# Split-head attention followed by routed experts on one core: batch 2's outputs and routing pulled into batch 3, gathers placed behind their experts' weights

## The chip, the cores and the metric

The kernel runs on one core of a Trainium2 chip. The metric is the time of one execution in microseconds (us), measured on the device. The parts of a core that matter here are these: PE (matrix multiply), DVE (VectorE), ACT (ScalarE), POOL (GpSimd, which here issues all casting, gathering and scattering DMAs), and 16 DMA engines that all queues share (see the prediction's citation of the Trainium skill). "Half clock" below means a granted clock of 0.50 in the profile's clock record. A "gather" reads rows of HBM by an index table, a "scatter" writes rows back by one.

A run counts as slow when it is over 1.5% above the fastest run of its kernel. Single runs of one kernel differ by several per cent here, mostly with the clock that PE was granted. The kernel before took from 200.9 to 213.4 us within one job, at mean clocks from 0.96 down to 0.88. Ratios are taken inside one job, on fast runs.

## The reference

Four batches of 768 tokens and 8 heads of 64 go through causal attention. Heads 0, 2 and 6 see all earlier keys. The others see 4 sink keys and a window of 64. The 3072 tokens of 512 features then go through 8 experts:

```python
skip_score = x @ w_skip                 # tokens at or below 0 are passed through
logits = xc @ w_gate                    # 8 experts
e_idx = np.argmax(logits, axis=1)       # one expert a token
gate_w = softmax(logits)[e_idx]
for e in range(E):
    h = np.maximum(xc[mask] @ w1[e], 0.0)       # 512 x 1024
    y[mask] = gate_w * (h @ w2[e])              # 1024 x 512
out[do_compute] = xc + y
```

## The kernel before

The attention output is written to `out` in HBM. Each expert has two slots of 128 tokens (t = 0, 1). Slot 0 is filled from batches 0 to 2 and slot 1 last. A slot's rows are gathered from `out` by an index table, computed, and scattered back. Attention runs batch by batch in six "slots" of work; the outputs of batch b-1 (`"o"`) and their transposes and gates (`"x"`) are interleaved with the scores of batch b.

```python
def trans(b, pr):                       # queries and keys of one pair of heads
    ...
    eng = nc.scalar.copy if name == "qT" and b else nc.vector.tensor_copy
    eng(t..., ps...)                    # PSUM -> SBUF
    ...
    elif pr:                            # small product for the sink keys: reads the key copy
        nc.vector.tensor_tensor(y..., t..., half, op=ALU.mult)

def outp(g):                            # output block g; one bank `av` until batch 3
    avo = oview(sp.tile(...) if g >= g0 else av)
    ...                                 # PE, then DVE divides, then SP stores to `out`

def route(c0):                          # a generator: go_on() runs its next stage
    ...                                 # DVE: maximum, one-hot `oh`, ...
    yield
    rp = tp.tile(sh, FP32, tag="t", name="rps")
    ...                                 # PE: rank matmuls, read `oh`
    yield ...                           # DVE: rank; POOL: product; PE: table `tb`; DVE: idg, idx

# experts, in order of issue on POOL
#   4 gathers t=0 | w2[3], w1[4], w2[4] | 4 gathers t=1 | w1[5] | gathers of 4 | w2[5]
#   | gathers of 5, 6, 7 | w1[6] | w2[6], w1[7] | w2[7] | scatters
```

The scatters are declared free of order among themselves. A scatter still waits for every gather issued earlier, because both use `out`.

The softmax here doesn't subtract the row's maximum and nothing guards it: scores larger than these inputs give would overflow.

## Time and profile before

| | before |
|---|---|
| median of the runs beside the changed kernel | 204.38 us (201.17 to 205.56, 4 runs) |
| profiled span, mean granted clock | 204.6 us, 0.950 |
| PE busy | 163.1 us (80%) |
| batch 3's first exponential | 75.23 us |
| first expert matmul | 121.94 us |
| last PE matmul ends | 194.9 us |
| first, last scatter issued | 160.58, 195.96 us |

PE and the DMA engines are both nearly full, and the tail behind PE's last matmul is 9.7 us. The views are in the prediction. A row of a timeline gives start, duration, engine, line, operation, output <- input, and in brackets how long the engine stood idle before it and what released it.

### The profile page before, as it was taken

To read this page: it belongs to the slowest core of one execution; us is meant where nothing else is said; L and a number is where in the kernel's file an instruction comes from. 1 tells how busy PE (TensorE), PEld (TensorE's weight loads), DVE (VectorE), ACT (ScalarE), POOL (GpSimd) and SP (SyncE) were. 2 spreads that over 40 slices of the span, in tenths; PEclk is the share of its full clock that TensorE was granted. 3 is DMA by queue.
4 is the path that set the end of the run, shared out by engine and by line. 5 is a ranking of instruction groups with operands and counts; after the bars stand their busy time and mean duration, and the time that the engine had idled before them with its cause. 6 is when DMAs were issued, how large, how long until landed. Compare 5 with 4: busy or idle time off the path is not lost. (4 is left out here: it accounts for less than half of the span.)

```text
span 204.6 us, 5665 instructions
## 1 busy us (share of the span) xinstructions
PE 163.1 (80%) x2422; PEld 116.7 (57%) x2422; DVE 111.9 (55%) x282; ACT 83.5 (41%) x116; POOL 85.1 (42%) x105
## 2 busy tenths in 40 slices
PE   5898878967788687886898688959988959999900
PEld 1455556746566565664777558648755727657400
DVE  5888877554957849574683626233345344344410
ACT  2067788855874558746121133212322422232000
POOL 8659711421861218412014801687632451145430
PEclk9999999999999999999669889988999999999985
DMA  5999999999899999999999899999999999942010
GB/s 164 174 172 157 180 196 214 222 181 229 139 182 228 240 216 246 225 190 243 215 235 272 222 171 238 208 302 239 239 258 181 208 210 211 278 155 79 23 67 3
DMA packets 53172, 39.97 MB, mean 195 GB/s; under 512 B 27976, under 2 KB 44360, under 8 KB 53136
## 3 DMA queue, kind: packets, MB, share of 16 engines
q0 software_dynamic: 49136, 32.43, 104.2%
q1 hardware_dynamic: 3728, 6.69, 9.7%
q8 instruction: 21, 0.34, 0.6%
q10 hardware_dynamic: 272, 0.39, 0.5%
q14 instruction: 15, 0.12, 0.2%
HBM read 56.66 MB, written 10.49 MB: 328 GB/s over the span
## 5 line engine op out<-in xcount | busy, mean ns | idle before, releaser
L433 POOL CAST x<-x 128x512 f16<-128x512 f32 x17 | 10.7, 627 | 43.3 <-DVE x L426 37.4
L344 ACT ACTIVATE at<-sps 128x1024 f16<-128x1024 f32 (+1 forms) x24 | 21.7, 918 | 11.6 <-PE sps L333 11.1
L685 POOL DMA_INDIRECT out_dram<-xg,idx x16 | 16.0, 1001 | 24.0 <-DVE xg L748 10.6
L731 PE MATMUL mhp<-mxT,w1t 128*128 128x128 f16 (+1 forms) x320 | 24.4, 238 | 0.7 <-ACT mxT L717 0.7
L731 PEld LDWEIGHTS <-w1t 128*128 128x128 f16 x320 | 22.6, 103 | 3.5 <-issue 1.1
L735 DVE TENSOR_SCALAR ht<-mhp 128x512 f16<-128x512 f32 x16 | 11.1, 691 | 23.3 <-PE mhp L731 20.3
L746 PE MATMUL myp<-w2t,ht 128*128 128x512 f16 x96 | 23.6, 380 | 0.0
L748 DVE SCALAR_TENSOR_TENSOR xg<-myp,tab,xg 128x512 f32<-128x512 f32 x16 | 12.0, 751 | 19.6 <-PE myp L746 18.2
L679 POOL DMA_INDIRECT xg<-out_dram,idg x16 | 16.4, 1025 | 10.5 <-DVE tab L536 4.8
L737 ACT ACTIVATE ht<-mhp 128x512 f16<-128x512 f32 x16 | 9.6, 597 | 26.5 <-PE mhp L731 21.1
L383 ACT ACTIVATE ats<-sps 128x1024 f16<-128x1024 f32 (+1 forms) x16 | 12.3, 808 | 14.6 <-PE sps L374 14.6
L746 PEld LDWEIGHTS <-ht 128*128 128x128 f16 x128 | 12.0, 99 | 10.3
L439 PE MATMUL xps<-ident,x 128*128 128x128 f16 (+1 forms) x96 | 12.9, 263 | 6.0 <-ACT qT L302 2.4
L302 DVE COPY kT<-tps 128x768 f16<-128x768 f16 x16 | 15.2, 951 | 3.5 <-PE tps L296 3.5
L333 PE MATMUL sps<-qT,kT 64*128 64x512 f16 (+3 forms) x96 | 15.1, 308 | 0.0
L328 PE MATMUL sps<-tri,idl 64*128 64x128 f16 x144 | 11.4, 221 | 3.3 <-ACT ats L383 2.7
L717 ACT COPY mxT<-mtp 128x512 f16<-128x512 f16 x11 | 6.2, 587 | 17.7 <-PE mtp L714 16.8
L426 DVE TENSOR_TENSOR x<-av,rec 128x512 f32<-128x512 f32 x18 | 12.5, 692 | 1.4
L349 ACT ACTIVATE at<-sps 128x1024 f16<-128x1024 f32 (+1 forms) x12 | 10.8, 916 | 5.0 <-PE sps L333 4.8
L114 POOL DMA_DIRECT2D va<-in_v_dram x8 | 11.4, 1426 | 2.7 <-DMA va<-in_v_dram 1.2
L446 DVE COPY xT<-xps 128x512 f16<-128x512 f16 x17 | 7.6, 446 | 7.2 <-PE xps L439 7.0
L517 POOL TENSOR_TENSOR mv<-ot,vals 128x192 f32<-128x192 f32 (+1 forms) x4 | 2.5, 618 | 21.7 <-DVE ot L511 21.7
(152 smaller groups left out, 341.5 us busy)
## 6 DMA issues: line engine op xcount, KB each, us to landing
out_dram<-x SPq DMA_DIRECT2D x24, 256.0 KB, 5.8
w1t<-in_moe_w_dram POOLq DMA_DIRECT2D x6, 1024.0 KB
w2t<-in_moe_w_dram POOLq DMA_DIRECT2D x6, 1024.0 KB
va<-in_v_dram POOLq DMA_DIRECT2D x8, 384.0 KB
qin<-in_moe_w_dram POOLq DMA_DIRECT2D x2, 1024.0 KB
kin<-in_moe_w_dram POOLq DMA_DIRECT2D x2, 1024.0 KB
qin<-in_q_dram POOLq DMA_DIRECT2D x2, 768.0 KB
kin<-in_k_dram POOLq DMA_DIRECT2D x2, 768.0 KB
```

What stands on the lines that cost most here:

```text
L114: nc.gpsimd.dma_start(out=y[:, x, :D], in_=vr[b, :, x])
L302: eng(t.rearrange("c (p n) -> c p n", n=NT), ps.rearrange("c n p -> c p n"))
L333: nc.tensor.matmul(ps[:, k, x:x + n], kT[b, pr][rows[i], j * P:(j + 1) * P], qT[b, pr][rows[i], q0:q0 + n], start=False, stop=True, skip_g ...
L344: nc.scalar.activation(both[b][:, :, o:o + w], ps[:, :, :w], ACT.Exp, scale=SCALE)
L383: nc.scalar.activation(both[b, pr][:, :, x0:x1], ps[:, :, :x1 - x0], ACT.Exp, scale=SCALE)
L426: nc.vector.tensor_tensor(x.rearrange("p c t d -> p t c d"), avo[:, :, :, :D], rec.unsqueeze(3).to_broadcast([P, 2, 4, D]), op=ALU.mult)
L439: nc.tensor.matmul(ps[:, s], x[:, s * P:(s + 1) * P], ident if x.dtype == FP16 else ident32, is_transpose=True, start=(s == 0), stop=(s == ...
L679: nc.gpsimd.indirect_dma_start(out=xg[e, t], out_offset=None, in_=out[:n, :], in_offset=bass.IndirectOffsetOnAxis(ap=idg[:, t, e:e + 1], a ...
L685: sc = nc.gpsimd.indirect_dma_start(out=out[:, :], out_offset=bass.IndirectOffsetOnAxis(ap=idx[:, t, e:e + 1], axis=0), in_=xg[e, t], in_o ...
L731: nc.tensor.matmul(hp[:, u], wts[e, 0][:, s, (f0 + u) * P:(f0 + u + 1) * P], xts[n][:, s], start=(s == 0 and u == 0), stop=(s == DS - 1 an ...
L746: nc.tensor.matmul(yp, hts[n][:, f, i * P:(i + 1) * P], wts[e, 1][:, f], start=(f == 0), stop=(f == FS - 1))
L748: nc.vector.scalar_tensor_tensor(xg[e, t], yp, tab[:, t, e, 1:2], xg[e, t], ALU.mult, ALU.add)
```

## The change

The intent: have batch 2's routing done by the end of batch 3, so that the first gathers go out early, the bridge between attention and experts is shorter, and no scatter stands between weight loads. The diff, cut to its core:

```diff
@@ trans
-            eng = nc.scalar.copy if name == "qT" and b else nc.vector.tensor_copy
+            eng = nc.scalar.copy if b and (name == "qT" or pr > 1) else nc.vector.tensor_copy
@@ outp
-        avo = oview(sp.tile(...) if g >= g0 else av)
+        avo = oview(sp.tile(...) if g >= g0 and i % 3 else av)
@@ gates: two blocks at a time, through a transpose bank and a ScalarE copy into SBUF
+        nc.scalar.copy(lg[:, g - 1:g + 1], ps)
@@ slots
-            (C(0), "x", "o", C(1), T(1)),
-            (C(2), "x", "o", T(2), C(3)),
...
+        if b + 1 == B:
+            return (
+                (C(0), "x", "o", C(1), "o", T(1)),
+                (C(2), "x", "o", C(3), "g", "x", T(2), lambda: begin(g0 - 2 * NT)),
+                (C(4), "x", "o", go_on, C(5), "o", H6(0), "g", go_on),
+                (H6(2), "x", "o", H6(4), "g", T(3), A, "x", go_on),
...
@@ last slot of batch 0
+            (S4, "o", X(3, pair, 0, 512), T(0, b + 1), V(0, 1, 2, 3), X(3, pair, 512, S)),
@@ bridge: the fills go; experts:
-    for e in range(FB):                 # before the first expert's second group
-        gather(e, 1)
-    load_half(5, 0, *qk)
-    gather(4, 0) ... load_half(5, 1, *qk) ... gathers of 5, 6, 7
     for n in range(len(units)):
...
         down(n, lambda: xin(n + 2))
         if n == 0:
+            gathers t=1; load_half(4, 1); gathers of 4; load_half(5, 0); load_half(5, 1); gathers of 5
         if n == FB:
             load_half(FB + 2, 1)
+            gathers of 6
+        elif n == FB + 1:
+            load_half(FB + 3, 0); load_half(FB + 3, 1)
+            gathers of 7
         if n > FB:
             scatters()
```

## The prediction

> **What bounds the kernel now.** I read the page's slices first, then stretches of time, then the chain of waits, then each engine's timeline. Rows of the page's part 2 (40 slices of 5.1 us, in tenths):
>
> ```profile
> PE   5898878967788687886898688959988959999900
> ...
> PEclk9999999999999999999669889988999999999985
> DMA  5999999999899999999999899999999999942010
> ```
>
> Two resources are nearly full: PE until 195 us, and the 16 DMA engines until 180 us. The stretches put sizes on it (columns: from:to, length, busy us of PE, PEld, DVE, ACT, POOL with counts, granted clock, DMA share, GB/s):
>
> ```profile
> 52.00:56.00 4.00, 3.03 (x74) 2.22 (x70) 3.68 (x6) 3.35 (x5) 3.87 (x4) 1.00 0.70 111
> ...
> 72.90:99.40 26.50, 20.61 (x472) 16.09 (x464) 17.34 (x47) 16.06 (x20) 9.34 (x12) 0.99 1.41 224
> 99.40:121.90 22.50, 17.82 (x247) 14.44 (x242) 12.15 (x43) 5.07 (x10) 7.52 (x8) 0.78 1.04 221
> ...
> 120.00:180.00 60.00, 52.05 (x510) 38.36 (x509) 24.35 (x56) 16.41 (x29) 25.02 (x26) 0.97 1.13 234
> ```
>
> I split the span by PE's timeline: batch 3's scores end at 99.4; a bridge (last outputs, their transposes, gates, routing, fills) runs to 121.9; experts run to 194.9; a tail of 9.7 us ends at 204.6. Batch 3 leaves PE idle 26.5 - 20.6 = 5.9 us. The bridge leaves it idle 4.7 us and runs it at clock 0.78. The queue ran low once in attention (111 GB/s at 52 to 56 us).
>
> The chain of waits in the experts (start, us, what):
>
> ```profile
> 136.77 10.04 DMA xg<-out_dram,idg
> ...
> 147.11 12.61 DMA xg<-out_dram,idg
> ...
> 164.60 16.08 DMA out_dram<-xg,idx
> ...
> 180.70 0.43 DVE mx L702
> ...
> 187.99 6.92 PE myp L746 x32
> ```
>
> Gathers take 10 to 13 us to land because they queue behind weight loads, and the scatter issued at 164.6 landed at 180.7, behind the last of them. POOL's timeline gives the order of issue:
>
> ```profile
> 156.00 0.89 POOL L119 DMA_DIRECT2D w2t<-in_moe_w_dram  x1 [1.87 <-PE myp L746]
> 160.58 1.07 POOL L685 DMA_INDIRECT out_dram<-xg,idx  x1 [3.70 <-DMA xg<-out_dram,idg]
> 161.96 1.05 POOL L685 DMA_INDIRECT out_dram<-xg,idx  x1 [0.30 <-issue]
> ...
> 195.96 0.98 POOL L685 DMA_INDIRECT out_dram<-xg,idx  x1 [0.75 <-DVE xg L748]
> ```
>
> The first scatter waited for the last gather to land (147.11 + 12.61 = 159.7): a scatter overwrites the tensor that gathers read. Later ones follow every 1.31 us (181.24, 182.61, 183.90, 185.18, 186.47). This will matter.
>
> **What the Trainium skill says.** "TensorE: Matmul & The Clock Gate", part 1: the array falls to half clock after about 3.4 us of idleness and needs about as long a busy stretch to recover. The trace agrees in kind: clock 0.57 in 98 to 106 us, 0.58 in 116 to 120, 0.57 in 136 to 140, each some us after PE gaps (1.42 at 96, 1.60 at 112, 2.36 at 133), though the gaps are shorter than the figure. "DMA: Bandwidth & Descriptors", "Issuing engines are not separate DMA queues": all DMAs interleave on the same 16 engines; hence the share of about 1 whoever issues. "Perfetto Trace Analysis", "DMA Instruction — SWDGE (GPSIMD)": the profiled end is that of descriptor generation, not of the data. The trace agrees: a gather shows 1.0 us on POOL and lands 10 us later. I therefore reckon POOL's issue time and the queue's time apart.
>
> **The change part by part.**
> 1. Batch 2's outputs move into slots 0 to 3 of batch 3, its transposes, gates and whole routing up to the last table into batch 3. From the bridge go: one fp32 transpose of 4 matmuls (99.40 to 100.31, 0.9 us; now fp16, which takes 0.23 from start to next start), two gates (2 x 0.13) and the 0.70 wait between them, the rank matmuls (102.38 to 103.21, 0.83), and the 0.49 wait for POOL's product. Sum 3.2 us. The 12 fp32 table matmuls (1.3 us, 97.42 to 98.84) leave batch 3's end for batch 1's routing, but batch 2's stay in the bridge.
> 2. Fills go: 2 at 118.65 (0.78 to the next start), 4 at 120.91 (0.88), and the 0.73 wait for DVE before the latter, because the first expert's matmuls no longer stand behind it. Sum 2.4 us.
> 3. Batch 3 takes up about 0.2 + 0.8 + 0.5 = 1.5 us more PE work. It has 5.9 us of idleness, mostly waits for ACT's exponentials, so I let half be hidden: +0.8 us. DVE loses two key copies of 0.95 us per batch to ACT, where one takes 0.80; both have room in batch 3 (17.3 and 16.1 of 26.5), so I count zero.
> 4. Gates go through a transpose bank and a small ACT copy, two blocks at a time: 12 copies of about 0.2 us (my guess from the 0.24 us of ACT's smallest activation), off the path except for the last. Zero.
> 5. The bridge's remaining work, 6 outputs and 6 fp32 transposes, is unchanged, and so are most of the DVE and POOL latencies behind the four gathers there. Fewer gaps may save some half-clock time: about 4 us of PE work stood at half clock at 101.3 to 105.4. I take 0.7 us.
> 6. Experts: the second-pass gathers are issued after the first unit, and the gathers of experts 4 to 7 behind their own weights. PE's order per unit hardly changes: 73.0 us before, 72.3 after, since the 1.3 us of table matmuls stay and one of several DVE stalls may go.
>
> PE path: 121.9 - 3.2 - 2.4 + 0.8 - 0.7 = 116.4 for the first expert; + 72.3 = 188.7; + 9.7 = 198.4 us.
>
> 7. The new order on POOL makes a second path. The last gather now stands behind the last weight, and all scatters behind it. Bytes: before, 60 us at 234 GB/s (14.0 MB) between 120 and 180 carried all remaining loads, gathers and some 7 scatters of 0.26 MB (1.8 MB, 7.8 us). Without them the queue would be done at 172.2. The earlier load of v, issued at the end of a batch, fills the hole at 52 to 56 (worth 4 x (219 - 111)/219 = 2 us, with 219 GB/s in 56 to 96); a new hole before the second-pass gathers may cost some of it back. I put the last gather's landing at 170.5 us. Then 16 scatters: 0.84 us to the first, 16 x 1.31 = 21.0, last issue done at 192.3; from there to the end took 204.6 - 196.94 = 7.7 us. Sum 200.0 us.
>
> So PE gives 198.4 and scatters 200.0, close enough that the outcome is the later of two uncertain times. The median before is 0.4 above the profiled span. My figure is 199.5 us, 2.7% below 205.0.
>
> **The rivals.** (a) *Scatters become the bound outright.* For: all 16 wait for the last gather, and DMA has been full until 180. If the queue doesn't run ahead, the gather lands at 176 and the end is 205.5: nothing gained. Against: no scatter competes with loads any more. (b) *PE decides, and the clock improves.* If the half-clock stretches (16 us at 0.57 together, about 6.9 us lost) mostly vanish with the gaps, the end is near 194. Against: gaps beside POOL's descriptor work remain, and the second-pass gathers sit between experts. (c) *Batch 3 does not hide the added work*: v of batch 3 landed only at 95.1 us (DVE waited 2.62 us for it), and DVE's queue now has those copies earlier, ahead of the transposes' evacuations. A stall of 3 us there is possible: about 202. Against: v is requested 5 us earlier, though the queue ahead of it is as long. (d) *The expert's gather arrives late*: the cast of expert 7 stood at 180.7; 5.5 us earlier is 175.2, against a landing at 170.5. Only if the landing slips by 5 us does PE stop.
>
> **Range and chances.** The terms of the PE path are uncertain by some 3 us, the landing by 4 us, and single runs before spread from 201.17 to 205.56. Range 194.5 to 205. Faster by over 2% means under 200.9: 0.62. Slower needs over 209.1, which would take a stall beyond (a): 0.05. The rest, 0.33.
>
> **What would show it.** In the changed profile: PE's first expert matmul near 116 us; no 512-column fills in the bridge; the table of batch 2 on PE just after output 2 of batch 3, and the first gather on POOL near 104 rather than 109.5; DMA near 200 GB/s or more at 52 to 56; the first scatter on POOL near 171, an unbroken train of scatters every 1.31 us up to the end, and the last one later than PE's last matmul by more than 2 us. I am wrong if the experts start after 119, if batch 3 lengthens by over 2 us, if the scatter train starts before 166 or after 176, or if the expert phase takes other than 70 to 75 us.

## The result, and the profile after

The changed kernel took 214.12 us (median; 212.77 to 215.26, 4 runs) against 204.38 us. The ratio is 1.057, with a 95% interval of 1.042 to 1.073. A ratio here is the mean time of one kernel's fast runs over that of the other's of the same rounds, so it is not quite the ratio of the medians.

| us | before | after | difference |
|---|---|---|---|
| batch 1's first exponential | 28.32 | 30.09 | +1.8 |
| batch 2's first exponential | 49.94 | 51.71 | +1.8 |
| batch 3's first exponential | 75.23 | 80.77 | +5.5 |
| batch 3's last score matmul ends | 99.4 | 108.1 | +8.7 |
| first expert matmul | 121.94 | 121.94 | 0.0 |
| last PE matmul ends | 194.9 | 198.5 | +3.6 |
| end | 204.6 | 212.2 | +7.6 |

The bridge became shorter by 8.7 us, and attention longer by as much. That both kernels start the experts at 121.94 us to the digit is chance. The loss in the total lies behind the first expert matmul: 3.6 us in the experts and 4.0 us in the tail.

The page's slices of the changed kernel (5.3 us each, in tenths):

```profile
PE   5899498889869997878998789999996939599400
...
PEclk9999969999975599999579999999998888999975
DMA  6999999989999999999965899999999999334320
```

The clock now dips inside attention (slices 6, 12 to 14, 20 and 21), the queue runs low in the bridge (slices 21 and 22), and PE has holes late in the experts. The stretches, with the columns as in the prediction:

```profile
57.16:60.57 3.41, 1.46 (x35) 0.99 (x32) 1.38 (x8) 2.83 (x5) 1.98 (x3) 0.99 2.04 200
60.57:74.22 13.65, 13.65 (x180) 10.00 (x179) 6.75 (x20) 6.08 (x10) 2.31 (x4) 0.50 1.17 234
...
108.10:121.90 13.80, 11.66 (x222) 10.37 (x219) 8.39 (x26) 5.04 (x12) 6.64 (x7) 0.99 0.60 185
110.00:112.00 2.00, 1.84 (x31) 1.66 (x30) 1.97 (x5) 0.00 (x0) 0.69 (x1) 1.00 0.00 0
...
120.00:180.00 60.00, 52.07 (x505) 37.16 (x504) 24.18 (x56) 17.23 (x31) 20.48 (x22) 0.94 1.10 216
```

In 3.41 us PE was busy 1.46 us, a share of 0.43. The next 13.65 us it was busy all the time at a granted clock of 0.50, which by the clock is about half of what it can do in that time. The queue stood empty from 110 to 112 us.

This is the longest of several half-clock stretches. Before PE's last matmul they are, in the changed kernel, 26.4 to 29.8, 60.5 to 74.1, 101.5 to 108.3, 162.9 to 166.3 and 173.1 to 176.5 us, 30.7 us together. In the kernel before they are 98.9 to 105.7, 116.0 to 119.4 and 136.5 to 139.9 us, 13.7 us together. So attention lost 1.8 us in batch 0, whose last slot was reordered; 3.8 us in batch 2 (29.1 us long against 25.3); and 3.2 us in batch 3 (27.3 against 24.2). The 7 us stretch near 100 us falls in the bridge before and at the end of attention after, so it moves some of the time from one row of the table to the other.

What made the gap before 60.5 us is in the waits of DVE and of PE before 120 us (engine and line, what it waited for, us in total, times, longest):

```profile
DVE skq L311 <- ACT kT L305: 13.0, 6, 2.8
```

```profile
PE rps L494 <- DVE oh L483: 2.7, 2, 2.0
```

The key copy went to ACT, but the small sink-key product that reads it stayed on DVE. ACT was busy with exponentials, and in the trace DVE did nothing until the copy had been made, 13.0 us in six waits. The routing's one-hot came directly behind the product, and PE's rank matmuls behind that; their timelines have it in batch 2:

```profile
58.95 0.16 DVE L311 TENSOR_TENSOR skq<-kT,half 128x8 f16<-128x8 f16 x1 [2.18 <-ACT kT L305]
```

```profile
60.45 0.21 PE L494 MATMUL rps<-oh,utri 128*128 128x48 f16 x1 [1.95 <-DVE oh L483]
```

The order on POOL at the end:

```profile
155.97 0.81 POOL L119 DMA_DIRECT2D w1t<-in_moe_w_dram  x1 [3.48 <-DMA qin<-in_moe_w_dram]
161.27 1.11 POOL L119 DMA_DIRECT2D w2t<-in_moe_w_dram  x1 [4.49 <-DMA kin<-in_moe_w_dram]
...
164.06 1.03 POOL L706 DMA_INDIRECT xg<-out_dram,idg  x1 [0.31 <-ACT mxT L744]
...
185.38 1.04 POOL L712 DMA_INDIRECT out_dram<-xg,idx  x1 [20.29 <-DMA xg<-out_dram,idg]
186.72 1.02 POOL L712 DMA_INDIRECT out_dram<-xg,idx  x1 [0.31 <-issue]
...
204.82 0.98 POOL L712 DMA_INDIRECT out_dram<-xg,idx  x1 [0.30 <-issue]
```

The last gather, issued at 164.06, was still on its way when POOL began a wait of 20.3 us for it. Then the 16 scatters left without a break, one each (204.82 - 185.38) / 15 = 1.30 us. The last was issued 6.3 us after PE had ended (198.5). On DVE's timeline the experts wait for gathers too, which no cast did before:

```profile
172.74 0.43 DVE L729 CAST mx<-xg 128x512 f16<-128x512 f32 x1 [2.92 <-DMA xg<-out_dram,idg]
...
184.01 0.43 DVE L729 CAST mx<-xg 128x512 f16<-128x512 f32 x1 [1.64 <-DMA xg<-out_dram,idg]
```

Casts waited 6.4 us in all, in pairs for experts 5, 6 and 7. The pairs became free at 161.5, 172.7 and 184.0, so some 11.3 us apart: the time in which the queue moves two weight halves and two gathers, while PE needs 7.9 us for such an expert before (176.40 to 184.33). The late experts ran at the queue's pace.

### The profile page after: what moved, and what is told of

Read it like the earlier page. It is cut to its first block, busy times and chain, and to the rows that moved or that the text cites. A ratio compares the mean times of both kernels' runs of the same rounds, so it can differ in the third digit from the quotient of the medians.

```text
span 212.2 us, 5669 instructions
## 1 busy us (share of the span) xinstructions
PE 170.8 (81%) x2416; PEld 120.1 (57%) x2416; DVE 107.6 (51%) x277; ACT 89.1 (42%) x134; POOL 86.3 (41%) x106
## 5 line engine op out<-in xcount | busy, mean ns | idle before, releaser
L437 POOL CAST x<-x 128x512 f16<-128x512 f32 x18 | 11.5, 641 | 48.0 <-DVE x L430 25.8
L712 POOL DMA_INDIRECT out_dram<-xg,idx x16 | 15.8, 990 | 24.9 <-DMA xg<-out_dram,idg 20.3
L758 PE MATMUL mhp<-mxT,w1t 128*128 128x128 f16 (+1 forms) x320 | 22.9, 230 | 1.2 <-ACT mxT L744 1.2
L758 PEld LDWEIGHTS <-w1t 128*128 128x128 f16 x320 | 21.1, 98 | 3.9 <-issue 1.4
L762 DVE TENSOR_SCALAR ht<-mhp 128x512 f16<-128x512 f32 x16 | 11.1, 691 | 15.7 <-PE mhp L758 15.7
L336 PE MATMUL sps<-qT,kT 64*128 64x512 f16 (+3 forms) x96 | 16.4, 322 | 1.0 <-DVE kT L305 1.0
L430 DVE TENSOR_TENSOR x<-av,rec 128x512 f32<-128x512 f32 x20 | 13.8, 692 | 1.5
L443 PE MATMUL xps<-ident,x 128*128 128x128 f16 (+1 forms) x96 | 11.6, 250 | 2.5 <-ACT qT L305 1.5
L331 PE MATMUL sps<-tri,idl 64*128 64x128 f16 x144 | 12.5, 233 | 0.9 <-ACT at L347 0.8
L741 PE MATMUL mtp<-ident,mx 128*128 128x128 f16 x44 | 4.8, 238 | 8.7 <-DVE mx L729 8.7
L282 PE MATMUL av<-esk,ident 128*128 128x512 f16 x28 | 9.5, 470 | 2.6 <-DVE ident L142 1.8
L305 DVE COPY kT<-tps 128x768 f16<-128x768 f16 x10 | 9.5, 950 | 3.6 <-PE tps L299 3.4
```

The source lines that it names most:

```text
L331: nc.tensor.matmul(ps[:, k, x:x + P], idl[rows[i], u], tri[rows[i], u], start=(u == 0), stop=False, skip_group_check=True)
L336: nc.tensor.matmul(ps[:, k, x:x + n], kT[b, pr][rows[i], j * P:(j + 1) * P], qT[b, pr][rows[i], q0:q0 + n], start=False, stop=True, skip_g ...
L430: nc.vector.tensor_tensor(x.rearrange("p c t d -> p t c d"), avo[:, :, :, :D], rec.unsqueeze(3).to_broadcast([P, 2, 4, D]), op=ALU.mult)
L437: nc.gpsimd.tensor_copy(xs[g], xf)
L443: nc.tensor.matmul(ps[:, s], x[:, s * P:(s + 1) * P], ident if x.dtype == FP16 else ident32, is_transpose=True, start=(s == 0), stop=(s == ...
L712: sc = nc.gpsimd.indirect_dma_start(out=out[:, :], out_offset=bass.IndirectOffsetOnAxis(ap=idx[:, t, e:e + 1], axis=0), in_=xg[e, t], in_o ...
```

## The experiments

Three theories were put up. A: two causes, where late gathers set the end and the DVE stall with its half-clock stretch costs attention time that is partly hidden. B: the queue alone. C: the attention delay alone. Four kernels ran on one chip; the kernel before had a median of 204.07 us there (200.9 to 213.38, 8 runs). The changed kernel itself was not run again, so differences from it cross jobs.

**1. Key copies back on VectorE**

```diff
-            eng = nc.scalar.copy if b and (name == "qT" or pr > 1) else nc.vector.tensor_copy
+            eng = nc.scalar.copy if name == "qT" and b else nc.vector.tensor_copy
```

> The changed kernel with one line undone: the key copies of pairs 2 and 3 go back from ScalarE to VectorE. Theory A (two causes in series): in the changed kernel VectorE's tiny sink-key product stood 13.0 us in all waiting for ScalarE's key copy, with the routing behind it, which left the PE gap of 1.95 us at 60 us and the half-clock stretch of 61 to 75 us. Undone, batch 3's first exponential comes near 75 us instead of 80.8, the first expert matmul near 116 instead of 121.9; but the last gather still lands behind the last weight, so only some of it is kept: about 207 us. Theory B (the DMA queue alone sets the end, attention time is hidden): 211 to 214. Theory C (the attention delay alone): 205 to 206.

Measured: 212.19 us (211.35 to 214.12), ratio 1.054 (1.037 to 1.070). Batch 3 began at 73.73 us instead of 80.77, as theory A said. The first expert began at 118.99, only 3 us earlier and not near 116, since 20.5 us at half clock came in batch 3 instead:

```profile
82.10:85.50 3.40, 2.26 (x59) 1.96 (x57) 2.71 (x12) 1.54 (x3) 0.54 (x1) 1.00 1.25 244
85.50:106.50 21.00, 20.44 (x262) 15.00 (x259) 10.07 (x35) 8.54 (x14) 1.78 (x4) 0.51 1.47 212
```

The end moved by 1.9 us in the medians. That is theory B's number, and theory C falls. Theory A's 207 us was missed too, but as the new half clock took back most of the gain in attention, the run does not separate A from B.

**2. Gathers before the late weights**

```diff
             load_half(4, 1, *qk)
-            gathers of 4; load_half(5, 0); load_half(5, 1); gathers of 5
+            load_half(5, 0, *qk); gathers of 4; load_half(5, 1, *qk); gathers of 5, 6, 7
...
-            gathers of 6   (behind w2[6])
-            gathers of 7   (behind w2[7])
```

> The changed kernel with the gathers of experts 5, 6 and 7 issued before the weights of experts 5 (second half), 6 and 7, as the kernel before does; all else as changed. Theory A: first expert matmul still at 121.9 us, no wait of VectorE's cast for a gather, scatters start near 160 us instead of 185, PE's last matmul near 194 and the end near 204 to 205. Theory B: the same 204 to 205. Theory C: 212 to 214, as the end would follow the experts' start alone.

Measured: 207.56 us (206.99 to 207.77), ratio 1.028 (1.016 to 1.040). That is 6.6 us below the changed kernel's median in its own job, at the same clocks (0.911 to 0.919 against 0.907 to 0.922). Waits of casts for gathers fell from 6.4 to 0.4 us. PE ended at 192.7 and the end came at 205.6, so the tail was still 12.9 us. Theories A and B had the scatters start near 160 us and 204 to 205 us in all. POOL shows why it came out later:

```profile
167.99 1.06 POOL L712 DMA_INDIRECT out_dram<-xg,idx  x1 [5.73 <-DMA xg<-out_dram,idg]
...
187.92 0.98 POOL L712 DMA_INDIRECT out_dram<-xg,idx  x1 [4.07 <-DMA out_dram<-xg,idx]
...
198.25 0.99 POOL L712 DMA_INDIRECT out_dram<-xg,idx  x1 [0.30 <-issue]
```

The scatters begin 17.4 us earlier than in the changed kernel, then hold at 177.95, 182.87 and 187.92, 5 us apart, until the last weights are through. The remaining eight follow at 1.3 us each.

**3. Both undone**

> The changed kernel with both undone: key copies on VectorE and gathers before the late weights. Theory A: both gains are had, first expert near 116 us and no late gather: about 198 to 200 us, faster than the kernel before. Theory B: no better than with the gathers alone, 204 to 205. Theory C: 205.

Measured: 207.8 us (202.19 to 210.97), ratio 1.009 with an interval of 0.985 to 1.033. Two runs were slow at clock 0.90. The two fast ones were 202.19 and 205.14 us at 0.951 and 0.926. Unclear, and none reached theory A's 198 to 200 us. The profiled run was a slow one, and its time is not compared. It does show how far experiment 1 carries: with the same attention code it has half clock from 62.3 to 79.3 us, and its batch 2 took 30.1 us, against 23.0 us and none in experiment 1. A wait of 1.3 us at the rank matmuls was left in both. So the key copies' return does not by itself keep the clock up.

**4. The kernel before with late gathers**

```diff
-    load_half(5, 0, *qk); gather(4, 0); gather(4, 1); load_half(5, 1, *qk); gathers of 5, 6, 7
+    gather(4, 0); gather(4, 1); load_half(5, 0, *qk); load_half(5, 1, *qk); gathers of 5
...
             load_half(FB + 2, 1)
+            gathers of 6
             load_half(FB + 3, 0)
...
                 load_half(FB + 3, 1)
+                gathers of 7
```

> The kernel before with the changed order of gathers alone: experts 5, 6 and 7 gathered behind their own weights, so that all scatters stand behind the last weight. Attention and bridge untouched. Theory A and B: VectorE waits for gathers of experts 6 and 7, the first scatter issues near 180 us instead of 160.6, and the end comes 16 x 1.3 us and a tail later, near 208 to 211 us. Theory C: unchanged, about 204.

Measured: 209.07 us (204.72 to 215.7), ratio 1.036 from a single fast run, so the size is loose. Its profile (a fast run at clock 0.951) is plain, however:

```profile
176.16 1.03 POOL L685 DMA_INDIRECT out_dram<-xg,idx  x1 [20.64 <-DVE mx L702]
...
195.57 0.98 POOL L685 DMA_INDIRECT out_dram<-xg,idx  x1 [0.31 <-issue]
```

The profile names a DVE cast as what ended the wait of 20.64 us; the last gather had been issued at 154.36. PE ended at 189.2 and the end came at 202.9. The tail is 13.7 us, as in the changed kernel and 4.0 us more than before. The late gathers hardly held PE here, against the expectation (casts waited 0.2 us for gathers; PE waited 3.2 us once, at 137 us, for an earlier one), and it ended 5.7 us sooner than in the profile before. So the longer tail is that of the scatter train. Theory C falls again.

**5. Loads and batch 0 set back as well**

```diff
-        if n == FB:
-            load_half(FB + 2, 0)      # ahead of down(n)
-        if n == FB: load_half(FB + 2, 1)
-        elif n == FB + 1: load_half(FB + 3, 0); load_half(FB + 3, 1)
+        if n == FB - 1: load_half(FB + 2, 0)
+        elif n == FB: load_half(FB + 2, 1); load_half(FB + 3, 0)
+        elif n == FB + 1: load_half(FB + 3, 1)
...
-            (S4, "o", X(3, pair, 0, 512), T(0, b + 1), V(0, 1, 2, 3), X(3, pair, 512, S)),
+            (S4, T(0, b + 1), "o", X(3, pair, 0, 512), X(3, pair, 512, S), V(0, 1, 2, 3)),
```

> The run with both undone (keys on VectorE, gathers first), with two more parts set back: the weights of experts 6 and 7 are issued one expert unit earlier, as before, and the last slot of batch 0 has its transposes before the streaming scores, as before. What is left of the change is the order of outputs, transposes, gates and routing in batches 1 to 3 and the bridge. Theory A1 (the scatter train's end is set by when the last weights were issued, since scatters of the first units stall behind them): the last scatter follows PE's last matmul by about 1 us as in the kernel before, tail 9.7 us instead of 13, and batch 1 starts near 28.3 us instead of 30; 199 to 203 us in runs at clock 0.94 or more, 204 to 206 at 0.91. Rival A2 (the train is set by POOL's 16 x 1.3 us alone): no change, about 207.

Measured: 206.46 us (205.85 to 209.65) against 205.88, ratio 1.005 (0.999 to 1.012). The tail stayed at 12.9 us (PE's end 191.1, end 204.0): the first scatter left only at 166.31, since the gathers themselves were issued later than before (last one 153.70 against 147.11). The expectation A1 failed. Batch 3 began at 72.44 us, 2.8 us ahead of the kernel before, and then ran from 85.4 to 102.5 at half clock. Batch 1 began at 28.86 us instead of the changed kernel's 30.09, and the half-clock stretch at 26 us was gone. (Experiment 1, with the reordered slot but without that stretch, has 29.68.)

**6. Fills at the rank wait** (changed kernel)

```diff
-        rp = tp.tile(sh, FP32, tag="t", name="rps")
+        rpf = tp.tile([P, 512], FP32, tag="t", name="rps")
+        for _ in range(8 if c0 == 0 else 0):
+            nc.tensor.matmul(rpf, ident, fill, start=True, stop=True)
+        rp = rpf[:, :n * E]...
```

> The changed kernel with 8 dummy matmuls of 512 columns (about 0.22 us each) put on PE ahead of batch 0's rank matmuls in batch 2, where PE stood idle 1.95 us behind VectorE; nothing else changed. If the half-clock stretch of 60.5 to 74.5 us comes from that gap (the 3.4 us window 57.2 to 60.6 has PE busy 0.43[...]), the stretch goes and batch 3's first exponential comes near 77 us instead of 80.8. The end hardly moves by theory A, as the last gather and the scatter train set it: 210 to 213. If the stretch has another cause, it stays, and all times with it: 214.

Measured: 219.83 us (215.18 to 221.93), ratio 1.056 on its fast runs. The two stretches, and the later one:

```profile
57.16:60.57 3.41, 3.29 (x45) 1.92 (x43) 1.99 (x9) 2.43 (x5) 1.33 (x2) 1.00 1.79 207
60.57:74.22 13.65, 13.22 (x287) 10.53 (x284) 9.81 (x28) 9.11 (x15) 4.52 (x6) 1.00 1.16 241
86.00:107.00 21.00, 20.30 (x253) 14.98 (x253) 8.84 (x32) 8.93 (x15) 2.31 (x4) 0.51 1.52 210
```

With the gap filled by dummy work, the same 13.65 us ran at clock 1.00, with 287 matmuls instead of 180, and batch 3 began at 74.77 instead of 80.77 us (0.6 us of this came before batch 2). Experiment 2, which has the gap unfilled, had its stretch too (59.7 to 73.4 us). This speaks for the gap as the cause of that stretch, on one profile of a slow run. But batch 3 then had 20.5 us of it, and the total did not gain. The profile is of a slow run, which also had PE stalls behind 200 us that no other run shows; the total is not explained.

**7. The kernel before with keys on ACT**

```diff
-            eng = nc.scalar.copy if name == "qT" and b else nc.vector.tensor_copy
+            eng = nc.scalar.copy if b and (name == "qT" or pr > 1) else nc.vector.tensor_copy
```

> The kernel before with the key copies of pairs 2 and 3 on ScalarE, nothing else of the change. If this part alone makes the gaps, VectorE waits for ScalarE ahead of the sink-key product in each batch (2 to 3 us), half-clock stretches appear in attention, and the time is 3 to 6 us above the kernel before. If it only hurts together with the new place of the routing, which stands directly behind it in VectorE's order: within 1 us of the kernel before.

Measured: 205.98 us (204.09 to 208.74) against 205.88, ratio 1.001 (0.993 to 1.009). DVE's sink-key product waited 7.1 us for ACT in all, and it did not matter. This fits the expectation that the part hurts only where the routing stands directly behind it.

**8. Rank matmuls one score group later** (on experiment 5)

```diff
-                (C(4), "x", "o", go_on, C(5), "o", H6(0), "g", go_on),
+                (C(4), "x", "o", C(5), go_on, "o", H6(0), "g", go_on),
...
-            (C(4), "o", go_on, C(5), "x", H6(0), go_on),
+            (C(4), "o", C(5), go_on, "x", H6(0), go_on),
```

> The previous best (keys on VectorE, gathers first, weights and batch 0 as before) with the rank matmuls moved one score group later in batches 2 and 3, so that VectorE has finished the one-hot when PE comes to them. Without an experiment the last run had PE idle 1.3 us there in all, 0.67 us for the output bank beside it, and half clock from 85.5 to 102.5 us. Theory A: the waits at the rank matmuls fall below 0.3 us, the half-clock stretch in batch 3 goes or shrinks to 7 us, first expert near 113 to 116 us instead of 120.3; PE's last matmul near 185, but the scatter train still ends about 4 us behind it: 199 to 203. Rival: another gap (the output bank used twice in a row) takes its place and half clock stays 14 us or more: 205 to 207.

Measured: 207.5 us (206.49 to 211.83) against 208.21, ratio 1.003 (0.985 to 1.022). PE's wait at the rank matmuls went, but its wait for the output bank, used twice in a row, was 1.6 us, and half clock came from 84.8 to 101.8. The first expert began at 120.1 us and not at 113 to 116. The rival's number was right; that the bank is the cause is not shown.

**9. Gathers before the first expert's second matmul group** (on experiment 8)

```diff
     up_(1)
+    go_on()
+    gathers t=1; load_half(4, 1); load_half(5, 0); gathers of 4; load_half(5, 1); gathers of 5, 6, 7
     for n in range(len(units)):
```

> The same with the second-pass routing table and all remaining gathers issued before the first expert's second matmul group instead of behind it, as the kernel before does: the last gather issues some 3 us earlier and the scatters with it. Theory A: tail after PE's last matmul 10 to 11 us instead of 13, 2 us faster than the run with the rank matmuls later. Rival: [...]nothing is gained.

Measured: 205.56 us (199.31 to 211.33) against 208.21. The fast runs were 199.31 and 202.23, those of the kernel before 205.95, 208.04 and 205.09; the ratio of the means is 200.8 / 206.4 = 0.973, worked out here from few runs. The last gather was issued at 145.22 (154.24 in experiment 8, so something was gained, against the rival), the first scatter at 159.27, and the tail was 11.1 us instead of 13.0. In the profiled run half clock in batch 3 lasted only from 94.4 to 97.8 us. Its attention code is that of experiment 8, so a good part of this is luck, and the runs at clock 0.893 and 0.914 took 211.33 and 208.89 us.

**10. Doubled outputs apart** (on experiment 9)

```diff
-                (C(0), "x", "o", C(1), "o", T(1)),
+                (C(0), "x", "o", C(1), T(1), "o"),
...
-                (C(4), "x", "o", C(5), go_on, "o", H6(0), "g", go_on),
+                (C(4), "x", "o", C(5), go_on, H6(0), "o", "g", go_on),
```

> The last run's kernel with batch 2's doubled outputs set apart in batch 3 (the second output of slots 0 and 2 behind the transposes and the next score group), since two in a row share one output bank and PE waited 1.6 us in all for VectorE to empty it. Theory A (each PE gap removed lowers the chance that a 3.4 us window [...]is followed by half clock): the wait falls below 0.5 us, half clock between 75 and 105 us at most 4 us in most runs, 199 to 203 us with a smaller spread than 199.3 to 211.3. Rival (half clock comes by chance of the windows' phase whatever the gaps): the same spread, median 204 to 207.

Measured: 202.97 us (200.75 to 207.39, 6 runs) against 208.07 (204.56 to 214.23, 11 runs). The ratio is 0.975, with an interval of 0.959 to 0.992, so this version is faster than the kernel before by that interval, from three fast runs each. The wait for the output bank fell from 1.6 to 0.8 us, not below 0.5. The slices still have a dip in batch 3 (91 to 98 us) and one in the bridge:

```profile
PEclk9999999999999999996699669979999999999985
```

Half clock in batch 3 was 6.8 us rather than the 4 expected. The spread shrank from 12.0 to 6.6 us, which speaks for theory A but does not rule out luck: the two ran on different chips, with 4 and 6 runs.

**11. Fills too** (on experiment 10: 4 dummy matmuls before the rank matmuls in batches 2 and 3)

```diff
+        for _ in range(0 if last else 4):
+            nc.tensor.matmul(rpf, ident, fill, start=True, stop=True)
```

> The same with 4 dummy matmuls of 512 columns (0.9 us) ahead of the rank matmuls in batches 2 and 3. Theory A: where PE would wait they cost nothing[...]; elsewhere they cost up to 2 us in all; clock 0.94 or more in most runs, 200 to 204 us. Rival: 2 us slower than without them, at the same clock.

Measured: 204.23 us (203.03 to 205.03, 6 runs) against 208.07, ratio 0.991 (0.984 to 0.999). No run was below clock 0.937, and the spread was 2.0 us. The best runs lost about 2 us (203.03 against 200.75). Both halves of the expectation hold in part: fills steady the clock and cost time.

## Why the prediction was wrong

The prediction said 199.5 us, within 194.5 to 205, and gave slower by over 2% a chance of 0.05. The measured 214.12 us lies outside. All four of its "I am wrong if" came true: the experts started at 121.94 us, batch 3 lengthened by 3.2 us, the scatters started at 185.38 us, and the experts took 76.6 us. Its 205.0 us "median" was the profiled run's time; the median is 204.38 us.

**Step 7, the scatter path, had the right mechanism and a wrong size.** The wait for the last gather and then 16 scatters set the end, and the step 1.30 us was as predicted (1.31). The term that was mis-sized is "I put the last gather's landing at 170.5 us": the first scatter left at 185.38 and not 171.3. Experiment 2 against the changed kernel (6.6 us) and experiment 4 (tail 13.7 us) show that this order is what costs. The 14 us can be split roughly:

- Without the 7 scatters, the bytes moved in 120 to 180 us before were 60 x 0.234 - 1.8 = 12.2 MB. After, 60 x 0.216 = 13.0 MB moved there, and about 0.6 MB more came until 184.4 us (180 GB/s for two us, 105 for the rest). So 1.4 MB more was left to do at 120 us, worth 5.8 us at 234 GB/s, and the 2 us that I had credited for a filled hole were lost with it. The hole was filled (258 GB/s in 52 to 54 us), but 40 to 46 us had only 102 to 132 GB/s, and the bridge ran dry at 110, because the first gather came at 114.17 us and not near 104. It needed batch 2's table (ready at 113.9) and, by the profile, the stores of outputs to `out`, issued from 112.2 us on; most of the 10 us are attention's 8.7.
- The rate was 216 and not 234 GB/s: 60 x 18 / 234 = 4.6 us, and the last 0.6 MB took 4.4 us where 234 GB/s would take 2.6. POOL issued the last weight at 161.27 after a wait of 4.49 us for an older load to land. Why the rate was lower is not settled.

Rival (a) named this outcome, but stopped at a landing of 176 us; it came shortly before 185.4.

**Step 3, "DVE loses two key copies ... so I count zero", failed.** It counted busy time and not order. The copy's reader stayed on DVE, and DVE stood 13.0 us behind ACT. Together with the routing placed directly behind it, that opened a PE gap of 1.95 us, and 13.65 us of half clock followed. In experiment 7 the copy alone was harmless, and with the gap filled in experiment 6 the stretch was gone. The predicted +0.8 us for attention was +8.7. The gap lies in batch 2, which took 29.1 us against 25.3 before, and 23.7 with the gap filled. The rest, 1.8 us in batch 0 and 3.2 in batch 3, comes with half-clock stretches at 26.4 and 101.5 us, and why they came is open.

**Steps 1, 2 and 5, the bridge, gained more, but largely by the clock.** From the last score matmul to the first expert it took 13.8 us instead of 22.5, a gain of 8.7 against 6.3 predicted. The bridge before held 9.7 us of half clock, the one after 0.2 us. If work takes twice its time there, about 4.8 us of the gain are clock and 3.9 us are work removed (my estimate), against 0.7 and 5.6 predicted: steps 1 and 2 took several durations from inside the half-clock stretches of 98.9 to 105.7 and 116.0 to 119.4 us. The gain was used up by attention, so the first expert started at 121.94 us as before, and not at 116.4.

**Step 6, 72.3 us for the experts, was 76.6.** This is rival (d): the casts of experts 5, 6 and 7 waited 6.4 us for gathers. In experiment 2, with the gathers first, it was 71.4 us (121.35 to 192.7).

**Rival (b)** held that fewer gaps would save half clock. That came in the bridge (0.99 against 0.78), and the opposite in attention; over the whole run the mean clock fell from 0.950 to 0.908. **Rival (c)** expected trouble in batch 3 from the late v; it was the key copies that made DVE wait. Experiments 8 and 9 also had PE wait 1.6 us for the output bank used twice in a row.

What stays open: how much of the half clock is chance (in batch 3, experiments 8 and 9 have the same attention code, and 17.1 and 3.4 us of it in their profiles; in batch 2, experiments 1 and 3 have 0 and 17.1), and the lower rate of the queue.

## What to carry to other kernels

When all writers wait for the last reader, the place of that last reader in a full queue decides the end; put readers ahead of bulk loads, even when the data is needed late. When you move work between engines, look at who reads it and what stands behind that reader in its engine's order, not at busy shares. Here a PE gap of 1.95 us was followed by 13.65 us at half clock, so check the granted clock slice by slice before judging a reordering.

## What the Trainium skill lacked or had wrong

- "TensorE: Matmul & The Clock Gate", part 1: the page has a free-running window of 3413 ns and gives half clock after an idle window. The stretches here are multiples of it (3.41, 6.83, 13.65, 17.07 and 20.48 us), but the window before one need not be idle. One with PE busy 1.46 of 3.41 us came before 13.65 us of half clock, and one with 2.26 of 3.40 us before 20.5 us. The same page's section on cycling through PSUM banks does say that short idle gaps can do it, without a figure.
- No busy share decides it in these runs; a bound that I had assumed in three expectations does not hold. I laid windows of 3.41 us end to end from the start of each run's own stretches. A window with 3.00 of 3.41 us (experiment 11, from 90.5 us) came before half clock, and windows with 1.54 (experiment 4, from 135.4), 1.50 (experiment 9, from 125.1) and 2.06 us (the kernel before, from 54.5) did not. What else counts is open; PE's busy time is partly modelled, and which kinds of matmul fill the window was not tested.
- The same page, part 1: a busy window of about 3.4 us is said to bring the clock back. In the experts half clock lasted one window (3.41 us at 162.9 and at 173.1). In attention, PE was busy for 13.65 of 13.65 us by the profile and the clock stayed at 0.50.
- "DMA: Bandwidth & Descriptors": no section read here says that POOL stops issuing until older loads have landed; "Perfetto Trace Analysis" mentions a descriptor buffer that can fill up, but no such wait. Here loads waited 2.45, 3.48 and 4.49 us for earlier loads, and scatters held 5 us apart at 177.95, 182.87 and 187.92 (experiment 2), about as far apart as those at 170.45, 176.12 and 181.24 in the kernel before. That a full buffer is the reason is my reading; no run isolates it.
- No page read here gives the issue interval of a 128-row scatter: 1.30 us on POOL, so 16 of them take 21 us even when nothing else is in the way.
